# Batch 0 in four pieces, and the set-up work in another order, in a fused convolution and mixer kernel

## The chip, the cores and the metric

The kernel runs on one core of one Trainium2 chip. A core has TensorE (PE in the profile, its weight loads PEld), VectorE (DVE), ScalarE (ACT), GpSimd (POOL) and a queue for transfers (SP). The time is device microseconds of one launch; a figure for a kernel is the median of several runs.

## The reference

x has 8 batches of 4224 rows and 192 columns. The first half is a causal convolution with 7 taps; the taps of each of 8 heads (24 columns) are a softmax of its weights:

```python
w = np.exp(w - max(w)); w = w / (sum(w) + 1e-9)        # [8 heads, 7 taps]
out = np.einsum('hk,bskhg->bshg', w, x_unf)            # x_unf: the 7 rows up to s
```

The second half mixes over the rows with a low-rank product and then over the columns with two dense layers:

```python
xt = x.transpose(0, 2, 1)
h = xt @ U @ V                                         # rank 32 over the 4224 rows
u = x + h.transpose(0, 2, 1)
ch = np.maximum(u @ w_ch1, 0.0) @ w_ch2                # 192 -> 768 -> 192
return u + ch
```

Here x of the second half is the output of the first. U has 4224x32 values, V 32x4224.

## The kernel before

A batch is 33 tiles of 128 rows. In SBUF its rows lie as bf16 in two halves of the partitions (x_sb): blocks of 64 rows, 32 of them on partitions 0 to 63 (r=0) and 34 on 64 to 127 (r=1), so that tile j of a half is two neighbouring blocks. The loads convert from float32 and are all issued from GpSimd's queue.

**The convolution** is a matmul with a banded matrix. From weight the kernel makes the softmax c_sb, multiplies it with the mask hot (where the difference of row and column equals a tap), adds the seven taps by matmuls with an identity (band_half, lines 221 to 244), and copies the sums into band. conv (L368) then takes, for some heads, row halves and tiles k0 to k1, two matmuls per block (the block itself and the one before it) and evacuates the sum into y_sb by ACT ("A") or DVE ("D"), both at helper lines L272 and L274. From batch 2 on conv32 does the same with 32-row pieces and needs a shifted copy of x (xb_sb, x_shift), which GpSimd makes piece by piece.

**The low-rank part.** tt is U transposed times y: tt_mm (L403) adds 33 products, four side by side in the array; tt_split and tt_sum add the four parts with the matrix R4. h_group multiplies V with it and adds y to give u_sb; transp transposes u_sb by a transfer. **The dense part** runs over 33 groups of 8 tiles: w1 (L590) with a Relu evacuation into rl_sb, w2 (L614) with the addition of u and the store.

**The start.** Nothing of the dense part can begin before tt of batch 0 is whole. Batch 0's x comes in two pieces, KP = [(0, 13), (13, 17)] in tiles of each half, two loads per piece. GpSimd's queue, in order: piece 0, the iotas (dif four times, tap, fp, efp), U (Ur), piece 1, V0, four loads of W1, five of V, W2. U arrives as four rows side by side and is unfolded by 16 matmuls with the selection Eq (u_layout). TensorE's order: sixty matmuls of zeros (idle), the two band halves, thirty more of zeros, the convolution of piece 0 head by head, u_layout, yT_part(0) (the transposed y of group 0), tt_first (26 products, and U4_sb, the rest of U copied four times side by side by DVE), the convolution of piece 1, a float32 product that adds the four parts (R4f, L701), tt_more (7 products with U4_sb, L451), tt_done, hT_part, and then the first group of w1. Groups 0 and 1 get their transposed input from yT_part and hT_part rather than from a transfer. R4f, R4 and Eq are made on DVE after the band products (lines 250 to 265). After this start the order is written out in SLOTS: groups for w1, groups for w2, and what is done at which step of w2 (c: convolution of heads, x: shifted copy, t and s: tt and its sum, h: a group of u). Loads of later batches are held back to given points (LOADS).

Two lines carry the order of the start:

```python
    for h in range(0, H, 4):
        conv(0, h, 4, [0, 1], "AD", *KP[1])
```

Of the kernel before, what the change touches and what calls it, by code (L numbers as in the profile page):

```python
# [14 lines left out]
def kernel(  # L15
# [40 lines left out]
    def bank():  # L56
        return psp.tile([P, 512], F32, name="ps", tag="ps")
# [28 lines left out]
    KP = [(0, 13), (13, NB1 // 2)]  # L86

    def x_piece(k):
        for r in range(2):
            k0, k1 = KP[k]  # L90
            k1 = min(k1, (NB0, NB1)[r] // 2)
            x_part(0, r, (1 - r if k == 0 else 2 * k0 + 1), 2 * k1 + 1)

    x_tile(0)
    x_piece(0)
# [5 lines left out]
    dif = cst.tile([P, BW], F32, name="dif")  # L101
    for r in range(4):
        nc.gpsimd.iota(
            dif[QB * r : QB * r + QB, :],
            pattern=[[1, BW]],
            base=0,
            channel_multiplier=-1,
            allow_small_or_imprecise_dtypes=True,
        )
    tap = cst.tile([P, KC], F32, name="tap")  # L110
    nc.gpsimd.iota(
        tap[:],
        pattern=[[-1, KC]],
        base=HW,
        channel_multiplier=0,
        allow_small_or_imprecise_dtypes=True,
    )

    fp = cst.tile([P, P], I32, name="fp")
    nc.gpsimd.iota(fp[:], pattern=[[1, P]], base=P, channel_multiplier=-1)  # L120

    efp = cst.tile([P, 4, P], I32, name="efp")
    nc.gpsimd.iota(efp[:], pattern=[[-1, 4], [1, P]], base=4 * P, channel_multiplier=-4)
# [11 lines left out]
    x_piece(1)  # L135


    V0_sb = cst.tile([32, 2 * GT * P], BF16, name="V0_sb")
# [9 lines left out]
    NSL = (NT + 7) // 8 * 2  # L148
    V_sb = cst.tile([P, NSL, P], BF16, name="V_sb")
    full = NT // 8  # L150
    for q in range(4):
        src = moe_V[:, 0 : full * 8 * P].rearrange("r (k q t) -> r k q t", q=4, t=2 * P)
        nc.gpsimd.dma_start(
            out=V_sb[32 * q : 32 * q + 32, 0 : 2 * full, :].rearrange(
                "r (k a) t -> r k (a t)", a=2
            ),
            in_=src[:, :, q, :],
        )
    assert NT % 8 == 1
    nc.gpsimd.dma_start(  # L160
        out=V_sb[0:32, 2 * (NT // 8), :], in_=moe_V[:, (NT - 1) * P : NT * P]
    )
    W2_sb = cst.tile([P, MC, D], BF16, name="W2_sb")
    nc.gpsimd.dma_start(out=W2_sb[:], in_=moe_w_ch2[:].rearrange("(m p) d -> p m d", p=P))


    zz = cst.tile([P, 512], BF16, name="zz")
    nc.vector.memzero(zz[:])  # L168

    def idle(n, w):  # L170
        wps = bank()
        for _ in range(n):
            nc.tensor.matmul(  # L173
                out=wps[:, 0:w], lhsT=zz[:, 0:P], rhs=zz[:, 0:w], start=True, stop=True
            )

    idle(60, P)
# [3 lines left out]
    band = cst.tile([P, H, P], BF16, name="band")  # L181
    nc.vector.memzero(band[:])
    x_zero(0, nc.vector)
    hot = cst.tile([P, KC, BW], BF16, name="hot")
    nc.vector.tensor_tensor(
        out=hot[:],
        in0=dif[:].unsqueeze(1).to_broadcast([P, KC, BW]),
        in1=tap[:].unsqueeze(2).to_broadcast([P, KC, BW]),
        op=ALU.is_equal,
# [11 lines left out]
    nc.scalar.activation(e_sb[:], d_sb[:], ACT.Exp)  # L201
    ident = cst.tile([P, P], BF16, name="ident")
# [16 lines left out]
    HQ = H // 2  # L219

    def band_half(hh):
        pr = sml.tile([P, KC, HQ, BW], BF16, name="pr")
        nc.vector.tensor_tensor(
            out=pr[:],
            in0=hot[:].unsqueeze(2).to_broadcast([P, KC, HQ, BW]),
            in1=c_sb[:, :, HQ * hh : HQ * hh + HQ].unsqueeze(3).to_broadcast([P, KC, HQ, BW]),
            op=ALU.mult,
        )
        bp = bank()
        for d in range(KC):  # L230
            nc.tensor.matmul(
                out=bp[:, 0 : HQ * BW],
                lhsT=ident[:],
                rhs=pr[:, d, :, :],
                start=(d == 0),
                stop=(d == KC - 1),
            )
        for r in range(4):
            o = QB * (r % 2)
            nc.scalar.activation(  # L240
                out=band[QB * r : QB * r + QB, HQ * hh : HQ * hh + HQ, o : o + BW],
                in_=bp[QB * r : QB * r + QB, 0 : HQ * BW].rearrange("p (h t) -> p h t", h=HQ),
                func=ACT.Copy,
            )

    band_half(0)
    band_half(1)
# [4 lines left out]
        out=efp[:], in0=efp[:], scalar1=P - 1, scalar2=None, op0=ALU.bitwise_and  # L252
    )
    nc.vector.tensor_scalar(
        out=Eq[:], in0=efp[:], scalar1=0.0, scalar2=None, op0=ALU.is_equal
    )
# [7 lines left out]
    R4 = cst.tile([P, P], BF16, name="R4")  # L264
    nc.vector.tensor_copy(out=R4[:], in_=R4f[:])

# [9 lines left out]
    def u_layout():  # L276
        up = [bank() for _ in range(4)]
        nb = [nfull + (1 if 32 * jj < nlast else 0) for jj in range(4)]
        for a in range(4):
            for jj in range(4):  # L280
                nc.tensor.matmul(
                    out=up[jj][:, 0 : nb[jj] * R],
                    lhsT=Eq[32 * jj : 32 * jj + 32, a, :],
                    rhs=Ur[32 * jj : 32 * jj + 32, 0 : nb[jj], a * R : (a + 1) * R],
                    start=(a == 0),
                    stop=(a == 3),
                    tile_position=(32 * jj, 0),
                )
        for jj in range(4):
            evac(  # L290
                "AD"[jj % 2],
                U_sb[:, 0 : nb[jj], jj, :],
                up[jj][:, 0 : nb[jj] * R].rearrange("p (k r) -> p k r", r=R),
            )

# [38 lines left out]
    def conv32(b, h0, nh, engs):  # L334
# [5 lines left out]
        for n in range(nh):  # L340
# [3 lines left out]
            for cg in range(4):  # L344
                t, w, st = (
                    (xt[b], band[:, h, QB : 2 * QB], 1 + cg // 2)
# [21 lines left out]
    def conv(b, h0, nh, rs, engs, k0=0, k1=NT):  # L368
# [4 lines left out]
        pp = {r: bank() for r in rs}  # L373
        w = nh * GS
        for hh in range(nh):
            h = h0 + hh
            for halo in range(2):
                for r in rs:
                    for c in range(2):
# [5 lines left out]
                            lhsT=band[HB * r : HB * r + HB, h, HB * halo : HB * halo + HB],  # L385
# [42 lines left out]

    def tt_first(p, js, rest):


        U4_sb = cst.tile([P, sum(b - a for a, b in rest), 4, R], BF16, name="U4_sb")
        n = 0
        for a, b in rest:
            nc.vector.tensor_copy(
                out=U4_sb[:, n : n + b - a, :, :],
                in_=U_sb[:]
                .rearrange("p k j r -> p (k j) r")[:, a:b, :]
                .unsqueeze(2)
                .to_broadcast([P, b - a, 4, R]),  # L440
            )
            n += b - a
        p = tt_mm(0, js, p, 256)
        t = sml.tile([P, D], F32, name="tt_f", bufs=1)
        evac("A", t[:], p[:, 256 : 256 + D])
        return U4_sb, t

    def tt_more(p, U4_sb, rest):
        js = [j for a, b in rest for j in range(a, b)]
        for n, j in enumerate(js):  # L450
            nc.tensor.matmul(  # L451
                out=p[:, 0:D],
                lhsT=U4_sb[:, n, :, :].rearrange("p a r -> p (a r)"),
                rhs=yt[0][:, j, :],
                start=False,
                stop=(n + 1 == len(js)),
            )
# [84 lines left out]
    def yT_part(g):  # L542

        tp = [bank() for _ in range(3)]
        for c in range(3):
            for i in range(4):
                for hf in range(2):
                    nc.tensor.matmul(
                        out=tp[c][HB * hf : HB * hf + HB, i * P : (i + 1) * P],
                        lhsT=yt[0][:, GT * g + 4 * hf + i, HB * c : HB * c + HB],  # L550
                        rhs=ident[:],
                        start=(i == 0),
                        stop=False,
                        tile_position=(0, HB * hf),
                    )
        return tp

    def hT_part(g, tp, engs):

        uTt[g] = uts.tile([P, 4, 3, P], BF16, name="uT")  # L560
        for c in range(3):
            for hf in range(2):
                nc.tensor.matmul(
                    out=tp[c][HB * hf : HB * hf + HB, :],
                    lhsT=ttb[0][0:32, HB * c : HB * c + HB],
# [4 lines left out]
                )  # L570
            for n, eng in enumerate(engs):
# [90 lines left out]
    for k in range(5, 14):  # L662
# [3 lines left out]
        if k < 10:  # L666
# [21 lines left out]
    idle(30, P)  # L688
    for h in range(H):
        conv(0, h, 1, [0, 1], "AD", *KP[0])  # L690
    u_layout()
    yT = yT_part(0)
    jb = NB0 // 2
    rest = [(KP[1][0], jb), (jb + KP[1][0], NT)]
    ps0 = bank()
    U4_sb, tf = tt_first(
        ps0, list(range(KP[1][0])) + list(range(jb, jb + KP[1][0])), rest
    )
    for h in range(0, H, 4):
        conv(0, h, 4, [0, 1], "AD", *KP[1])  # L700
    nc.tensor.matmul(out=ps0[:, 0:D], lhsT=R4f[:], rhs=tf[:], start=True, stop=False)  # L701
    tt_more(ps0, U4_sb, rest)
# [7 lines left out]
    for r in range(4):  # L710
        q = slice(QB * r, QB * r + QB)
        nc.gpsimd.tensor_copy(
            out=band2[q], in_=band[q, :, HB * (r % 2) : HB * (r % 2) + QB]
        )
# [84 lines left out]
```

## Time and profile before

| | before |
|---|---|
| median of 7 runs | 330.98 us (329.92 to 332.28) |
| the profiled execution | 332.14 us |
| its span, first to last instruction | 330.1 us |
| TensorE busy | 319.3 us, 97% of the span |
| DVE busy | 268.5 us, 81% |
| ACT busy | 171.3 us, 52% |
| GpSimd busy | 142.0 us, 43% |
| first matmul of the first convolution | 11.43 us |
| tt_done of batch 0 (DVE L461) | 19.22 to 19.58 us |
| first matmul of w1 (L590) | 20.96 us |

The busy share is an average over stages with different limits; a matmul counts as busy until its modelled end, so a full TensorE row says that matmuls follow one another, not that each is as fast as can be. Rows of the timeline give the start, the busy time of a run of equal instructions, engine, line, output and input with their shapes and the number; in brackets the idle time before and what ended it. In the rows of a stretch each engine has its busy time and number of instructions, in the order PE, PEld, DVE, ACT, POOL; then come the granted TensorE clock, the share of the DMA engines, and GB/s.

### The profile page before, as it was taken

What the parts mean: (1) busy time and instruction counts of PE and PEld (TensorE: products, weight loads), DVE (VectorE), ACT (ScalarE), POOL (GpSimd) and SP (SyncE); (2) the same over time, 40 slices, a digit from 0 to 9 for tenths busy, and PEclk for the clock granted to TensorE, in tenths of its full rate; (3) what the DMA queues carried; (4) which work ended last, traced back from release to release, by engine and by line L of the source; (5) the groups of instructions that cost most, each with busy time, mean ns of one, the idle gap of its engine ahead of it and who ended that gap; (6) DMA issues with size and microseconds to landing.
All of it is one profiled execution on the core that took longest, in us unless ns stands there. A gap on an engine that the chain in (4) does not pass through costs nothing.

```text
span 330.1 us, 9736 instructions
## 1 busy us (share of the span) xinstructions
PE 319.3 (97%) x4072; PEld 223.8 (68%) x4072; DVE 268.5 (81%) x547; ACT 171.3 (52%) x351; POOL 142.0 (43%) x109
## 2 busy tenths in 40 slices
PE   6889999999999999999999999999999999999995
PEld 6645666667646845877784695587787487487495
DVE  5746998996985998798699789879897898896863
ACT  1648454563496088248609806842912912912910
POOL 8580329663995785969569599000000000000000
PEclk9979999999999999999999999999999999999998
DMA  8999996699999799799989979039659359249035
GB/s 101 192 171 141 172 211 149 132 185 136 286 196 182 168 177 184 163 230 155 226 180 161 188 185 224 21 114 230 83 99 228 106 124 229 82 112 271 4 120 169
DMA packets 122908, 53.54 MB, mean 162 GB/s; under 512 B 87760, under 2 KB 122832, under 8 KB 122864
## 3 DMA queue, kind: packets, MB, share of 16 engines
q1 hardware_dynamic: 84672, 38.18, 52.3%
q0 software_dynamic: 38192, 14.73, 40.3%
q8 instruction: 32, 0.52, 0.7%
q14 instruction: 12, 0.10, 0.1%
HBM read 29.49 MB, written 25.95 MB: 168 GB/s over the span
## 4 chain that ended last, share of the span: by engine, by line
PE 78%; POOL 9%; DMA 7%; DVE 2%; ACT 1%; issue 1%; POOLq 0%
PE ps L614 37%; PE ps L590 33%; DMA x_sb<-in_x_dram 6%; POOL xb_sb L318 5%; PE ps L352 3%; PE ps L496 3%; POOL x_sb L79 2%; PE ps L411 2%; ACT rl_sb L601 1%; DMA V_sb<-in_moe_V_dram 1%; DVE y_sb L274 1%; POOL xb_sb L306 1%; DVE rl_sb L603 1%; PE ps L467 0%; DVE uT L274 0%
## 5 line engine op out<-in xcount | busy, mean ns | idle before, releaser
L601 ACT ACTIVATE rl_sb<-ps 128x512 bf16<-128x512 f32 x235 | 125.5, 603 | 112.2 <-PE ps L590 100.2
L614 PE MATMUL ps<-W_sb,rl_sb 128*128 128x192 bf16 x1584 | 141.7, 246 | 0.2
L614 PEld LDWEIGHTS <-rl_sb 128*128 128x128 bf16 x1584 | 128.0, 98 | 13.4 <-issue 12.8
L590 PE MATMUL ps<-uT,W_sb 64*128 64x512 bf16 x1188 | 133.5, 380 | 0.7 <-DVE uT L274 0.7
L603 DVE TENSOR_SCALAR rl_sb<-ps 128x512 bf16<-128x512 f32 x161 | 104.3, 687 | 19.2 <-PE ps L590 18.9
L590 PEld LDWEIGHTS <-W_sb 64*128 64x128 bf16 x1188 | 64.5, 95 | 65.5 <-issue 6.6
L622 DVE TENSOR_TENSOR out_sb<-ps,u_sb 128x384 f32<-128x384 f32 (+1 forms) x133 | 70.1, 548 | 25.0 <-PE ps L614 23.5
L318 POOL COPY xb_sb<-x_sb 32x3072 bf16<-32x3072 bf16 (+1 forms) x24 | 67.6, 2824 | 0.7
L518 DVE TENSOR_TENSOR u_sb<-y_sb,ps 128x192 bf16<-128x192 bf16 (+1 forms) x168 | 66.2, 459 | 0.0
L306 POOL COPY xb_sb<-x_sb 128x3072 bf16<-128x3072 bf16 x12 | 32.7, 2742 | 29.4 <-PE ps L352 15.9
L272 ACT ACTIVATE y_sb<-ps 128x384 bf16<-128x384 f32 (+3 forms) x90 | 36.8, 502 | 10.1 <-PE ps L352 7.9
L79 POOL DMA_DIRECT2D x_sb<-in_x_dram x32 | 27.0, 851 | 29.1 <-PE ps L590 17.1
L274 DVE CAST y_sb<-ps 128x408 bf16<-128x408 f32 (+2 forms) x42 | 20.8, 547 | 3.3 <-PE ps L381 2.3
L496 PE MATMUL ps<-tt_sb,V_sb 32*128 32x192 bf16 x264 | 12.6, 246 | 0.8 <-DVE tt_sb L461 0.6
L352 PE MATMUL ps<-xb_sb,band 64*32 64x384 bf16 x192 | 12.4, 332 | 0.8 <-POOL xb_sb L318 0.8
L352 PE MATMUL ps<-x_sb,band 64*32 64x384 bf16 x192 | 12.1, 333 | 0.0
L496 PEld LDWEIGHTS <-V_sb 32*128 32x128 bf16 x264 | 4.7, 92 | 8.2 <-issue 8.2
L352 PEld LDWEIGHTS <-band 64*32 64x32 bf16 x384 | 4.6, 89 | 5.1 <-issue 4.0
L173 PE MATMUL ps<-zz 128*128 128x128 bf16 x90 | 6.8, 248 | 1.2 <-DVE zz L168 1.2
L425 ACT ACTIVATE tt_hi<-ps 128x192 bf16<-128x192 f32 x7 | 2.3, 331 | 10.8 <-PE ps L411 10.8
L381 PE MATMUL ps<-x_sb,band 64*64 64x312 bf16 (+3 forms) x192 | 7.2, 277 | 0.2 <-DMA x_sb<-in_x_dram 0.2
L173 PEld LDWEIGHTS <-zz 128*128 128x128 bf16 x90 | 6.5, 114 | 1.2 <-DVE zz L168 1.2
(64 smaller groups left out, 71.8 us busy)
## 6 DMA issues: line engine op xcount, KB each, us to landing
out_dram<-out_sb SPq DMA_DIRECT2D x131, 192.0 KB, 3.0
x_sb<-in_x_dram POOLq DMA_DIRECT2D x14, 384.0 KB, 7.9
x_sb<-in_x_dram POOLq DMA_DIRECT2D x7, 432.0 KB, 7.9
x_sb<-in_x_dram POOLq DMA_DIRECT2D x7, 408.0 KB, 7.9
x_sb<-in_x_dram POOLq DMA_DIRECT2D x1, 648.0 KB, 9.5
x_sb<-in_x_dram POOLq DMA_DIRECT2D x1, 624.0 KB, 7.1
uT<-u_sb SPq DMA_TRANSPOSE x31, 4.3
W_sb<-in_moe_w_ch_dram POOLq DMA_DIRECT2D x2, 192.0 KB, 5.8
```

The lines of the kernel that those rows point to most:

```text
L79: return nc.gpsimd.dma_start(out=xt[b][HB * r : HB * r + HB, s0:s1, :], in_=x[b, blk * HB : (blk + s1 - s0) * HB, :].rearrange("(j p) d -> ...
L272: nc.scalar.activation(out=out, in_=in_, func=ACT.Copy)
L306: nc.gpsimd.tensor_copy(out=xbt[b][:, s0:s1, :], in_=xt[b][:, s0 + 1 : s1 + 1, :])
L318: nc.gpsimd.tensor_copy(out=xbt[b][q, s0:s1, :], in_=xt[b][q, s0:s1, :])
L352: nc.tensor.matmul(out=pp[r][QB * cg : QB * cg + QB, 0 : nk[r] * GS], lhsT=w[hr], rhs=t[hr, st : st + 2 * nk[r] - 1 : 2, hs], start=True, ...
L496: nc.tensor.matmul(out=banks[pr][:, a * D : (a + 1) * D], lhsT=V_sb[32 * q : 32 * q + 32, (j // 8) * 2 + j % 2, :], rhs=ttb[b][32 * q : 32 ...
L518: nc.vector.tensor_tensor(out=u_group(g)[:, i : i + n, :, hf, :], in0=yt[b][:, run[0] : run[0] + n, :].rearrange("p n (c k) -> p n c k", c=3),
L590: last = nc.tensor.matmul(out=pp[hf][:], lhsT=W1_sb[HB * hf : HB * hf + HB, c, m * P : (m + 1) * P], rhs=uTt[g][HB * hf : HB * hf + HB, :, ...
L601: nc.scalar.activation(out=rl[:, m, hf, :], in_=pp[hf][:], func=ACT.Relu)
L603: nc.vector.tensor_scalar_max(out=rl[:, m, hf, :], in0=pp[hf][:], scalar1=0.0)
L614: nc.tensor.matmul(out=cps[:, a * D : (a + 1) * D], lhsT=rlt[g][:, m, hf, (i + a) * P : (i + a + 1) * P], rhs=W2_sb[:, m, :], start=(m == ...
L622: nc.vector.tensor_tensor(out=o[:, 0:n, :].rearrange("p n (c k) -> p n c k", c=3), in0=cps[:, 0 : n * D].rearrange("p (n c k) -> p n c k", ...
```

## The change

- Batch 0's x comes in four pieces, each of one half: 10 tiles of r=0, 10 of r=1, then 7 of r=1, then 6 of r=0. The first two are loaded at once and convolved together, two heads per evacuation; each later one by itself, three heads per evacuation, into PSUM banks that are named (work).
- Idle matmuls: five of 128x512 in float32 at the start and one between the band halves, instead of sixty and thirty of 128x128 in bf16.
- Set-up: one dif iota and an addition of 32 per row quarter instead of four iotas; hot is made after d_sb; efp is float32 and Eq compares it with a number per partition (rq); Eq and R4f are made on DVE between the products of the bands and the rest; the bands are two tiles, the second one's copies are DVE's.
- U4_sb (now 13 tiles) and R4 are made by GpSimd after u_layout, and the loads of V and W2 come behind them on GpSimd's queue.
- tt of batch 0: 20 products four side by side, then 7 late ones, the R4f product, 6 late ones. yT_part makes two of its three chunks before the later pieces and the third after the late products.
- In slot 5 the convolution of batch 3, the shifted copy of batch 4, t3 and s3 come one step of w2 later. band2 is copied in eight parts instead of four.

The core of the diff:

```diff
-    KP = [(0, 13), (13, NB1 // 2)]
+    KP = [(0, 0, 10), (1, 0, 10), (1, 10, NB1 // 2), (0, 10, NB0 // 2)]
...
-    for r in range(4):
-        nc.gpsimd.iota(
-            dif[QB * r : QB * r + QB, :],
...
+    dif = cst.tile([P, BW], F32, name="dif")
+    iota(dif[:], [[1, BW]], 0, -1)
...
-    zz = cst.tile([P, 512], BF16, name="zz")
+    zz = cst.tile([P, 512], F32, name="zz")
...
-    idle(60, P)
+    idle(5)
...
+    nc.vector.tensor_scalar(
+        out=dif[:], in0=dif[:], scalar1=rq[:, 0:1], scalar2=None, op0=ALU.add
+    )
...
-            nc.scalar.activation(
-                out=band[QB * r : QB * r + QB, HQ * hh : HQ * hh + HQ, o : o + BW],
...
+            evac(
+                "AD"[hh],
+                bands[hh][QB * r : QB * r + QB, :, o : o + BW],
...
+    band_half(0)
+    idle(1)
+    band_half(1)
...
+        if k == 5:
+            at = {
+                2: ["c3:0:3:AAD"],
+                3: ["c3:3:3:AAD"],
+                4: ["c3:6:2:A", "x4:3"],
+                5: [hs[0]],
+                6: ["t3"],
+                8: ["s3", hs[1]],
+                11: [hs[2]],
+            }
...
+    for h in range(0, H, 2):
+        conv(0, h, 2, [0, 1], "AA" if h == 0 else "AD", *KP[0][1:])
+    work = [bank() for _ in range(4)]
+    u_layout(work)
+    o = 0
+    for js in late:
+        nc.gpsimd.tensor_copy(
+            out=U4_sb[:, o : o + len(js), :, :],
...
+    nc.gpsimd.tensor_copy(out=R4[:], in_=R4f[:])
...
+    yT = yT_part(0, (0, 1))
+    ps0 = bank()
+    conv_piece(2, work[0:3])
+    conv_piece(3, [work[3], work[0], work[1]])
+    tt_mm(0, piece_tiles(0) + piece_tiles(1), ps0, 256)
+    tf = sml.tile([P, D], F32, name="tt_f", bufs=1)
+    evac("A", tf[:], ps0[:, 256 : 256 + D])
+    tt_late(ps0, late[0], 0, True, False)
+    nc.tensor.matmul(out=ps0[:, 0:D], lhsT=R4f[:], rhs=tf[:], start=False, stop=False)
+    tt_late(ps0, late[1], len(late[0]), False, True)
+    yT_part(0, (2,), yT)
     tt_done(0, ps0)
     hT_part(0, yT, "AD")
```

tt_late is the loop of tt_more for a part of the tiles; conv_piece calls conv for one half:

```python
    def conv_piece(k, pps):
        r, k0, k1 = KP[k]
        for n, h in enumerate(range(0, H, 3)):
            conv(0, h, min(3, H - h), [r], "AD"[n % 2], k0, k1, {r: pps[n]})
```

## The prediction

> **What bounds the kernel.** I read the strip of slices first, then the chain of waits, then stretches of the start.
>
> ```profile
> PE   6889999999999999999999999999999999999995
> DVE  5746998996985998798699789879897898896863
> ACT  1648454563496088248609806842912912912910
> PEclk9979999999999999999999999999999999999998
> ```
>
> TensorE is full from the third slice on; in the stretch 105:326.3 it is busy 221.24 of 221.30 us. From 105 us on nothing but its own instructions counts, and the change leaves these alone (batches 4 to 7, all groups). The change can act in two places only: until the first W1 matmul (L590, 20.96 us), and at a wait of TensorE before 105 us in slot 5. What the first W1 matmul gains, the end gains, since the evacuation-bound stretches at 30 and 41 us move along with it.
>
> The chain up to there:
>
> ```profile
> 5.28 0.86 POOL Ur L130
> 6.14 0.53 POOL Ur L134
> 6.67 0.65 POOL x_sb L79
> 7.32 8.44 DMA x_sb<-in_x_dram
> 15.76 0.28 issue
> 16.05 0.54 POOL V_sb L153
> 16.58 3.04 DMA V_sb<-in_moe_V_dram
> 19.63 0.42 PE ps L563 x2
> ```
>
> The reader sees batch 0's last rows land at 15.76. The V_sb step is how the view orders releasers; hT_part at 19.63 starts when tt_sb is written (DVE L461, 19.22 to 19.58), after the last late product of batch 0. So what ends last is: x lands, convolution, products with U, tt_done.
>
> **Part 1, the first piece and the bands.** It shrinks from 13+13 to 10+10 tiles: 53 blocks of 64 rows to 41. As bf16 in SBUF a block is 24.6 KB, so 0.295 MB less at the 190 GB/s of the slices from 4.5 us on: 1.55 us. Its second half landed at 11.94 (TensorE waits 0.19 us for it there), so now about 10.3. The bands must be as early. Before, hot waited until 4.60 for the four dif iotas; one iota is left (0.65 us less), and hot moves behind d_sb, where DVE would wait for ACT's exp. The first pr goes from 6.71 to about 5.9 and ends at 7.1. The first half's seven products and four ACT copies (2.45 us for eight) end at 9.2 to 9.7; the second half's copies go to DVE and end near 11, when heads 4 to 7 are wanted. So the convolution starts at 10.3 instead of 11.94.
>
> What could take that back stands ahead of the band products in TensorE's order: five float32 matmuls of 128x512 instead of sixty bf16 ones of 128x128 (4.94 us). The nearest row is
>
> ```profile
> 17.76 0.59 PE L701 MATMUL ps<-tt_f,R4f 128*128 128x192 f32 x2
> ```
>
> with the next matmul 0.54 us after its start, at full clock. It has two records of at least 326 ns, against 246 ns for one bf16 matmul of 192 columns: 80 ns of streaming more each, so twice the columns per record. By that streaming 512 columns need 4 x 512 columns, 0.85 us; with the weight loads (two of 0.19 us, partly hidden) about 1.0. Scaled by columns whole, 1.44 is the other bound. The granted clock reads 1.00 from the start, but 29 of the sixty short matmuls fill the 3.01 us up to 4.21 and the other 31 take 1.93 us: 104 ns and 62 ns each, so about half rate until 4.2 us. At 1.0 the five end at 7.7 (1.4 to 4.2 us hold 1.4 of them), at 1.44 near 9.9. I take 1.0. The cover is x's landing: ends up to about 8.8 cost nothing, after that microsecond for microsecond.
>
> **Part 2, from there to tt_done.** The first convolution has 8 evacuations of 480 columns instead of 16 of 312. ACT's eight of 312 took 2.69 us and eight of 384 2.69+0.50=3.19, so 0.875 ns a column and 0.48 us each; DVE (3.21 us for eight of 312, 3.99 for eight of 408) 0.57. Five on ACT end at about 13.4; u_layout runs under them, its four evacuations (0.38 to 0.41) end at 14.1; yT for two of three chunks (16 at 28 ns) stands in between; piece 2 (7 tiles of the second row half) runs 14.0 to 15.1, its x due about 13.6. Then TensorE waits for piece 3. Piece 3 is the last of batch 0's x; all bytes ahead of it are those of before (pieces and U, 1.87 MB), so it lands where the last landed before: 15.2 (bytes over the slices' rate, plus 0.9 us from last byte to landing) to 15.76. I take 15.6. **This is the point of the whole start:** TensorE gains 1.6 us at the front and meets the same landing.
>
> From there, in TensorE's order:
> - piece 3: 32 matmuls of 144 columns, two side by side in the array (one half of the rows). yT's 24 of 128 columns took 0.86 us, 28 ns apart; so 31 ns, 1.0 us
> - 20 products with U, four side by side: the 26 of L411 are 22 ns apart, 0.44 us
> - seven late products: L451's are 95 ns apart, 0.67; tt_f's evacuation (0.33, and 0.4 of latencies around it) lies beside them. It reads the PSUM bank that they write; no row of before shows the two together. If they wait for it, 0.65 more; I take nothing, as their columns differ (0 to 191, 256 to 447)
> - the float32 R4f product 0.54, six late products 0.57, then latency of the last and start of DVE, 0.25.
>
> Sum 3.5 us: tt_done at 19.1, against 19.22 before. There x was already there when TensorE was still at yT and the first products (until 16.95), and only 7 late products came after it; now 13 do, and the whole of piece 3. Gain 0.1; by the landing (15.2 to 15.76) and the shared bank between 0.5 gained and 0.8 lost. yT's third chunk, 0.2 us, lies under tt_done.
>
> **Part 3, GpSimd.** U4 (7+6 tiles, 128 columns each) goes from DVE (0.35 and 0.28 us for 3 and 4 tiles) to GpSimd, and R4 with it. Row: a 3072-column bf16 copy takes 2742 ns there, 0.89 ns a column, so 1664 columns 1.5 us plus R4 0.25. The skill's "GPSIMD Engine Reference", section Key points, says that elementwise work is about twice as fast on DVE: from DVE's 0.63 us for 7 tiles, 1.2 for 13, the rule gives 2.4. By the row the copies end at 15.9, by the rule at 16.8; the late products start at 17.1. Hidden by both; past 17.1 each microsecond counts. But behind them on GpSimd's queue stand five V loads, W2 (0.88 us) and batch 1's x. V starts at 16.0 instead of 14.18. Until 18.5 the DMA engines still work off W1, so they don't run dry; V is first used at 28.3, W2 at 33.5, x of batch 1 at 41.95, whose landing goes from 31 to at most 33. Costs nothing. band2 in eight copies is first used at 71 us. Eq and R4f stand between the band products on DVE, 0.5 us and ready long before u_layout.
>
> **Part 4, slot 5.** The convolution of batch 3 moves back by one W2 step.
>
> ```profile
> 97.07 3.08 POOL L318 COPY xb_sb<-x_sb 32x3456 bf16<-32x3456 bf16 x1
> 100.20 0.33 PE L352 MATMUL ps<-xb_sb,band 64*32 64x408 bf16 x1 [0.78 <-POOL xb_sb L318]
> ```
>
> TensorE arrived at 99.09 and waited 0.78 us for GpSimd's last shifted copy. A W2 step (12 matmuls) takes 1.10 us, so it now arrives at about 100.2, when the copy is done: 0.78 gone. Next late is the tile sums, which keep their two steps from t to s and three to the group that needs them; the shift for batch 4 starts 1.1 us later and GpSimd has 3.21 us idle at 113.4. Gain 0.78, bounds 0.5 to 0.8.
>
> **The clock.** A second term lies in the start:
>
> ```profile
> 17.86:21.28 3.42, 2.40 (x17) 1.22 (x18) 1.86 (x6) 1.33 (x5) 3.42 (x6) 1.00 1.21 142
> 21.28:24.69 3.41, 3.41 (x19) 1.41 (x18) 0.99 (x2) 1.68 (x3) 2.43 (x6) 0.50 1.59 190
> ```
>
> The eighth column is the granted clock: 0.50 for 3.41 us after a stretch with TensorE busy for 2.40 of 3.42, and twice the time for W1 there: 1.7 us lost. The Trainium skill, "TensorE: Matmul & The Clock Gate", section Why this matters for your kernels, asks for no idle gaps above some 3 us; no gap here reaches 1 us, so by it this term is zero, and the row says 1.7 us. Its Part 1 says that the window runs freely against the kernel's start, which fits the seven times: three at 329.9 to 330.5, one at 331.0, three at 332.0 to 332.3. The gaps about hT_part stay, less 0.2 us of yT, so I leave its frequency as it was and count from the median.
>
> **Sum.** The profiled execution took 332.14 us (span 330.1 and 2.0 around it). Less 0.1 and 0.78 it would be 331.3 with the lowered clock, 329.6 without. Against the median of 330.98: 330.98 - 0.88 = **330.1**.
>
> **Rivals.**
> - **Nothing gained, 330.9.** The landing of piece 3 at 15.8 or later, or the late products wait for tt_f. For: TensorE meets the same landing. Against: slot 5's wait is read from the trace and goes by itself. 14%.
> - **More gained, 329.0.** Piece 3 lands at 15.2 (0.5 us) and the lowered clock comes in fewer executions, a further 0.5 to 1.2 in the median. For: piece sizes and yT's filler; against: the gaps at 19.1 and 20.3 are unchanged. 20%.
> - **Slower, 333.0: the clock at the start.** The five float32 matmuls end after 8.8 us. If they do not raise the clock, each takes 1.9 us, they end at 10.9, the bands at 13, piece 3 follows at 17.8 instead of 15.6, and what follows runs at half rate for a while: +2.8, less 0.78. It decides from 9.8 us on (1.0 past the cover outweighs slot 5's gain). For: sixty plus thirty short matmuls kept TensorE busy until 11.3 and few remain; against: the array streams as densely in float32. 18%.
>
> **How the numbers follow.** The forecast has 48%, with its own range 329.1 to 331.3. A difference of about 0.5% (1.65 us) can be told from no change. Of the forecast's 48, 10 are below 329.33; with the second rival's 20 that gives 0.30 faster. Slower, above 332.63: 16 of the third rival and 1 of the forecast, 0.17. Same 0.53. The range from 328.6 to 332.5 leaves the worst of the third rival and a little of the second out.
>
> **What would show it.** TensorE's first convolution matmul at about 10.3; a wait for x before piece 3 near 15.1; tt_done at 19.1; W1 at 20.85; no wait for xb_sb at the convolution of batch 3; the five float32 matmuls over by 8 us. Wrong if W1 starts before 20.3 or after 21.5, or if TensorE gets a new wait after 21 us.

## The result, and the profile after

| | before | after |
|---|---|---|
| median | 331.10 us (61 runs, 329.69 to 333.17) | 329.71 us (24 runs, 329.38 to 331.12) |
| ratio after to before | | 0.9958, 95% interval 0.9944 to 0.9972 |
| profiled execution, its span | 332.14 us, 330.1 us | 330.22 us, 328.4 us |
| first matmul of w1 | 20.96 us | 20.27 us |
| from there to the end of the last matmul | 305.29 us | 303.30 us |
| from there to the landing of the last store | 1.97 us | 2.87 us |

The kernel is faster by 1.39 us, 0.42%, which is real but under 0.5%. The three lower rows are read from the traces' instruction and transfer records. The strip of slices of the kernel after:

```profile
PE   8989999999999999999999999999999999999994
DVE  6738999996978987898798799879888888896852
ACT  1758444662576198078429708824904903903900
PEclk9999999999999999999999999999999999999999
```

The first two slices of TensorE are fuller (8 and 9 for 6 and 8), and the clock has lost its 7 in the third. The rest is as before. The start in the timeline of the kernel after:

```profile
1.47 6.81 PE L155 MATMUL ps<-zz 128*128 128x512 f32 x10 [1.47 <-DVE zz L145]
8.11 0.62 PE L232 MATMUL ps<-pr,ident 128*128 128x152 bf16 x7
...
10.03 1.11 PE L367 MATMUL ps<-x_sb,band 64*64 64x240 bf16 x34
...
11.50 1.01 PE L367 MATMUL ps<-x_sb,band 64*64 64x240 bf16 x30 [0.36 <-DVE band L254]
...
13.60 2.27 PE L367 MATMUL ps<-x_sb,band 64*64 64x168 bf16 x64
...
14.17 1.69 POOL L683 COPY U_sb<-U_sb 128x896 bf16<-128x896 bf16 x2 [2.04 <-DVE U_sb L254]
...
15.81 0.29 POOL L691 CAST R<-R4f 128x128 bf16<-128x128 f32 x1
...
16.83 0.74 PE L664 MATMUL ps<-y_sb,U_sb 128*128 128x192 bf16 x7 [0.43 <-ACT tt_f L252]
...
18.52 0.36 DVE L419 CAST tt_sb<-ps 128x192 bf16<-128x192 f32 x1 [2.22 <-PE ps L664]
...
20.27 1.92 PE L550 MATMUL ps<-uT,W_sb 64*128 64x512 bf16 x14 [0.50 <-DVE uT L254]
```

The convolution starts at 10.03 and, in the row at 13.60, pieces 2 and 3 run as 64 matmuls in one go: TensorE waits for no x at all. Two new waits stand there, 0.36 us for the second band half and 0.43 us for tt_f. The chain of waits of the same execution, from its beginning, no longer holds a landing of x:

```profile
1.47 6.81 PE ps L155 x10
8.27 0.46 PE ps L232 x7
...
11.50 1.01 PE ps L367 x30
...
13.66 2.20 PE ps L367 x64
```

It starts at the float32 idle matmuls and runs to w1 through TensorE and evacuations. So the start is bound by something else than before, and the experiments come back to it. The stretches of the clock, at the same times as before:

```profile
17.86:21.28 3.42, 2.74 (x29) 1.33 (x28) 1.44 (x4) 0.94 (x3) 3.42 (x6) 1.00 0.80 83
21.28:24.69 3.41, 3.41 (x40) 1.68 (x36) 1.46 (x3) 3.35 (x7) 3.29 (x9) 1.00 1.49 175
```

TensorE is busy 2.74 instead of 2.40 us in the first, and the clock (eighth column) stays at 1.00 in the second. In slot 5, the timeline shows the last shifted copy over at 96.70 and the convolution running from 98.39 with no wait; before, the copy ended at 100.15 and TensorE waited 0.78 us:

```profile
93.62 3.08 POOL L303 COPY xb_sb<-x_sb 32x3456 bf16<-32x3456 bf16 x1
...
96.30 2.15 PE L574 MATMUL ps<-W_sb,rl_sb 128*128 128x192 bf16 x24
98.39 0.35 PE L337 MATMUL ps<-xb_sb,band 64*32 64x384 bf16 x2
```

One profile against the other, the difference is made of these parts: w1 starts 0.69 earlier; the lowered clock is absent, 1.71 (half of its 3.41); slot 5, 0.78; a new wait of 0.46 us for uT at 36.27, in this execution and not in the next one of the same kernel; and the last store, 0.90 later after the last matmul. The sum is -1.82 against -1.72 between the spans. The medians move by less, because before has the lowered clock only in some executions.

### The profile page after: what moved, and what is told of

The parts are those of the page before. It is cut to its first block, busy times and chain, and to the rows that moved or that the text cites. A ratio compares the mean times of both kernels' runs of the same rounds, so it can differ in the third digit from the quotient of the medians.

```text
span 328.4 us, 9588 instructions
## 1 busy us (share of the span) xinstructions
PE 319.0 (97%) x3994; PEld 221.0 (67%) x3994; DVE 268.9 (82%) x552; ACT 170.3 (52%) x346; POOL 143.8 (44%) x113
## 4 chain that ended last, share of the span: by engine, by line
PE 89%; DVE 5%; DMA 2%; ACT 2%; issue 0%; DVEq 0%
PE ps L574 40%; PE ps L550 37%; PE ps L337 3%; PE ps L454 3%; PE ps L155 2%; DMA uT<-u_sb 2%; PE ps L399 2%; ACT rl_sb L561 1%; DVE rl_sb L563 1%; DVE u_sb L476 1%; PE ps L367 1%; DVE y_sb L254 1%; DVE uT L254 0%; DVE band L254 0%; DVE out_sb L582 0%
## 5 line engine op out<-in xcount | busy, mean ns | idle before, releaser
L550 PE MATMUL ps<-uT,W_sb 64*128 64x512 bf16 x1188 | 132.0, 376 | 1.2 <-DVE uT L254 0.8
L291 POOL COPY xb_sb<-x_sb 128x3072 bf16<-128x3072 bf16 x12 | 32.7, 2743 | 29.6 <-PE ps L337 21.7
L252 ACT ACTIVATE y_sb<-ps 128x408 bf16<-128x408 f32 (+4 forms) x89 | 37.7, 512 | 10.1 <-PE ps L337 7.8
L254 DVE CAST y_sb<-ps 128x408 bf16<-128x408 f32 (+4 forms) x37 | 19.7, 577 | 1.0 <-PE ps L367 1.0
L155 PE MATMUL ps<-zz 128*128 128x512 f32 x12 | 7.9, 809 | 1.5 <-DVE zz L145 1.5
L367 PE MATMUL ps<-x_sb,band 64*64 64x240 bf16 (+3 forms) x192 | 7.8, 276 | 0.4 <-DVE band L254 0.4
L367 PEld LDWEIGHTS <-band 64*64 64x64 bf16 x192 | 5.9, 106 | 2.0 <-issue 1.0
```

The source lines that it names most:

```text
L252: nc.scalar.activation(out=out, in_=in_, func=ACT.Copy)
L291: nc.gpsimd.tensor_copy(out=xbt[b][:, s0:s1, :], in_=xt[b][:, s0 + 1 : s1 + 1, :])
L550: last = nc.tensor.matmul(out=pp[hf][:], lhsT=W1_sb[HB * hf : HB * hf + HB, c, m * P : (m + 1) * P], rhs=uTt[g][HB * hf : HB * hf + HB, :, ...
```

## The experiments

Each ratio is to the kernel before on the same chip, in the same set of runs. A profile is one execution; "W1" is its first w1 matmul, "body" the time from there to the end of the last matmul. In the kernel before the body is 303.6 us where slot 5 waits and the clock isn't lowered (305.29 - 1.71); without either it is 302.8. "Lowered" counts runs with a mean granted clock of 0.995 or less. One stretch of 3.41 us at 0.50 takes 0.005 off the mean over 330 us. The fall of the clock after the last matmul takes up to 0.004 (e2's profile, which has no such stretch, reads 0.996), so the two kinds of runs lie close, but hardly mix.

| kernel | median us (runs) | ratio, 95% | W1 | body | store after | lowered |
|---|---|---|---|---|---|---|
| c0, changed kernel again | 330.10 (12) | 0.9975, 0.9953 to 0.9998 | 20.35 | 302.86 | 2.91 | 0 of 12 |
| e1, its slot 5 undone | 330.14 (21) | 0.9966, 0.9950 to 0.9981 | 20.83 | 302.81 | 2.96 | 0 of 21 |
| e2, its yT whole and early | 330.09 (11) | 0.9953, 0.9934 to 0.9971 | 21.00 | 302.78 | 2.90 | 0 of 11 |
| e3, its tt_f in a bank of its own | 329.95 (14) | 0.9954, 0.9930 to 0.9978 | 19.52 | 302.79 | 2.78 | 1 of 14 |
| e5, its idle matmuls as before | 330.46 (12) | 0.9990, 0.9972 to 1.0008 | 21.64 | 302.81 | 2.46 | 0 of 12 |
| e6, sixteen idle DVE instructions more | 328.71 (12) | 0.9948, 0.9929 to 0.9966 | 21.09 | 302.80 | 1.93 | 0 of 12 |
| e8, e3 and e6 together | 329.15 (12) | 0.9951, 0.9930 to 0.9972 | 19.66 | 303.05 | 1.93 | 0 of 12 |
| e4, before with yT's third chunk late | 330.89 (22) | 0.9987, 0.9969 to 1.0004 | 21.80 | 303.63 | 1.96 | 0 of 22 |
| e7, before with wide idle matmuls | 335.16 (4) | 1.0102, 1.0072 to 1.0132 | 23.54 | 305.75 | 1.95 | 4 of 4 |
| e9, before with the new slot 5 | 331.68 (10) | 0.9994, 0.9970 to 1.0018 | 21.42 | 302.79 | 1.97 | 7 of 10 |
| e10, before with pieces 10 and 7 or 6 | 330.72 (10) | 0.9966, 0.9944 to 0.9987 | 21.26 | 303.45 | 1.97 | 0 of 10 |
| e11, before with eight idle DVE instructions | 330.43 (10) | 0.9973, 0.9947 to 0.9998 | 20.98 | 302.66 | 3.25 | 2 of 10 |

The kernel before itself had the lowered clock in 18 of 55, 13 of 35 and 14 of 25 runs of the three sets, 45 of 115 together. Its runs without it have medians of 330.75, 330.50 and 330.44 us; the first set goes with e1 to e4, the second with c0, e5, e6 and e8, the third with the rest.

c0 is the changed kernel once more, beside e5, e6 and e8 on one chip.

> The changed kernel once more, as the yardstick for the three others on the same chip: median 329.5 to 330.0. Its wait of 0.5 us for a transposed u at 36 us is either there again (then batch 1's later loads cause it) or not (then it is a matter of the single execution); its last store ends 2.8 to 3.0 us after the last matmul again if that belongs to the program.

It gave 330.10, and its profile shows the parts of above again: W1 at 20.35, no wait in slot 5, the last store 2.91 us after the last matmul; the wait for uT is not there. Against the runs of before without the lowered clock it gains 0.40 us (330.10 to 330.50). The parts in its profile give as much: 0.61 from W1 and 0.74 from the body, less 0.94 for the store, are 0.41.

### Slot 5: the move alone, and all but the move

e9 puts the new order of slot 5 into the kernel before; e1 takes the same lines out of the changed kernel.

```diff
-        if k < 10:
+        if k == 5:
+            at = {
+                2: ["c3:0:3:AAD"],
+                3: ["c3:3:3:AAD"],
+                4: ["c3:6:2:A", "x4:3"],
...
+        elif k < 10:
```

> The kernel before with slot 5's move alone. As predicted for the change: the wait of 0.6 to 0.8 us for xb_sb goes, from the first W1 matmul to the last matmul 302.8 us (303.6 before without a lowered clock), median 0.6 to 0.8 below before, 330.3. If a later step takes it back: the wait goes, that stretch stays at 303.6.

> The changed kernel with slot 5 as before (batch 3's convolution after the first W2 step). If slot 5's wait goes by the move alone: the wait for xb_sb is back at about 0.8 us in the profile and the median is 0.6 to 0.8 us above the changed kernel (330.4). If the shifted copies would have been in time anyway in the changed start: no wait, median 329.7.

e9: the body is 302.79, 0.8 us under the 303.6, and the wait is gone. The time does not show it: seven of its ten runs have the lowered clock, and the three others took 330.25, 330.38 and 330.58, where such runs of before have 330.44. That it was the move, and not an earlier copy, the traces show: the last copy ends 77.33 us after W1 in e9, and 77.53 and 77.35 in e4 and e10, where TensorE waits 0.64 and 0.46 us for it. The timeline of TensorE in e9 (w2 groups, then the convolution with no bracket):

```profile
96.94 2.16 PE L614 MATMUL ps<-W_sb,rl_sb 128*128 128x192 bf16 x24
99.03 0.35 PE L352 MATMUL ps<-xb_sb,band 64*32 64x384 bf16 x2
```

e1 missed: with slot 5 as before the wait did not come back. The last copy, a w2 group and the convolution in e1's timeline:

```profile
94.24 3.08 POOL L303 COPY xb_sb<-x_sb 32x3456 bf16<-32x3456 bf16 x1
...
96.82 0.82 PE L574 MATMUL ps<-W_sb,rl_sb 128*128 128x192 bf16 x8
97.57 0.35 PE L337 MATMUL ps<-xb_sb,band 64*32 64x384 bf16 x2
```

The copies follow the landing of batch 3's x (the copy over all 128 partitions, L291 there and L306 before, waits for it): that copy starts 59.1 us after W1 in e1 and 59.0 in the changed kernel, 59.9 in e9 and 61.8 before, of which 1.7 are the lowered clock. So in the changed kernel the x lands about a microsecond earlier against w1. The last copy ends 75.9 to 76.6 us after W1 in the eight profiles of it and its variants, and TensorE, in the old order, wants it at 76.7 (e1). Either cause removes the same wait: by the profiles the move is worth 0.8 us to the kernel before and nothing to the changed one. e11's profile, of the kernel before, has no such wait either (58.8 us).

Why the x comes earlier stays open, but the traces show what goes with it. The load of batch 3's last piece takes 11.5 to 11.9 us from issue to landing in before, e4, e9 and e10, and 9.1 to 10.8 in the ten other profiles. In those four a 16 KB instruction fetch of 1.9 to 2.4 us lies beside it, and in the ten others none is longer than 1.5. Whether the fetch holds up the load, or both are slow for one reason, is not shown.

### The lowered clock: what stands in the stretch before it

The changed kernel has more work for TensorE around tt_done: yT's third chunk, and thirteen late products instead of seven. e4 moves only the chunk, in the kernel before; e2 undoes only the chunk, in the changed one; e10 changes only the sizes of the pieces before, which makes thirteen late products (and takes three heads per evacuation of the second piece instead of four).

```diff
-    yT = yT_part(0)
+    yT = yT_part(0, (0, 1))
...
+    yT_part(0, (2,), yT)
     tt_done(0, ps0)
```

> The kernel before with one thing of the change: yT's third chunk after the late products. Theory clock: few or no executions with the lowered clock, spread 329.7 to 331 instead of 329.7 to 333.2, median about 330.3, 0.8 below before. Theory start: spread as before, median within 0.3 of 331.1.

> The changed kernel with all three chunks of yT made before the later pieces, so that nothing stands between the last late product and hT_part. Theory clock (the filled gap around hT_part keeps the clock up): some executions, up to half, have the clock at half for 3.4 us again, times spread up to 331.5, median 0.3 to 0.9 above the changed kernel. Theory start (the gain comes from earlier work alone): spread and median as the changed kernel, within 0.3, or up to 0.2 slower because yT's 0.2 us is no longer under tt_done.

```diff
-    KP = [(0, 13), (13, NB1 // 2)]
+    KP = [(0, 10), (10, NB1 // 2)]
...
-    for h in range(0, H, 4):
-        conv(0, h, 4, [0, 1], "AD", *KP[1])
+    for h in range(0, H, 3):
+        conv(0, h, min(3, H - h), [0, 1], "AD", *KP[1])
```

> The kernel before with pieces of 10+10 and 7+6 tiles alone (three heads per evacuation of the second). By the prediction's part 2 the smaller first piece meets the same landing of the last x and has 13 late products: W1 at 20.6 to 21.5, median within 0.5 of before. If the landing does not bind: W1 up to 0.7 earlier.

The lowered clock comes in 0 of 22 runs of e4 and 0 of 10 of e10, against 45 of 115 of the kernel before; e2 has none in 11. So the late chunk is enough by itself (e4), and so are the other piece sizes (e10), which bring the larger late part. The time shows no more than that: e4's 330.89 and e10's 330.72 are not below the 330.75 and 330.44 of before's runs without the lowered clock, and the 330.3 expected of e4 did not come. e4's lowest busy time over any 3.41 us of this part is 2.73, against 2.39 before; the row of stretches in e4:

```profile
18.39:21.80 3.41, 2.73 (x45) 1.61 (x34) 1.84 (x5) 1.59 (x5) 3.41 (x6) 1.00 0.97 108
```

The busy share alone does not decide, though. The clock changes in whole steps of 3.41 us from its rise: in the kernel before the lowered clock began five steps, 17.07 us, after the rise at 4.21, in e7 again 17.07, and in all fourteen traces the fall after the last matmul comes 94, 95 or 96 whole steps after the rise. Here are e2 and e10 in the stretch that these steps give, four after the rise:

```profile
18.78:22.20 3.42, 2.40 (x21) 0.99 (x20) 1.44 (x4) 1.07 (x4) 3.42 (x7) 1.00 0.89 96
```

```profile
18.24:21.66 3.42, 2.40 (x24) 1.44 (x23) 1.27 (x5) 0.94 (x3) 3.28 (x6) 1.00 1.14 124
```

Both are busy for 2.40 us as before was, and stayed at full clock afterwards (e9's 2.44 too). Stretches with less work did so as well, like the first one after the rise in the kernel before (1.93 us):

```profile
4.21:7.62 3.41, 1.93 (x34) 1.81 (x32) 2.67 (x9) 0.25 (x1) 3.34 (x8) 1.00 1.51 178
```

In e7 the stretch at 16.27, with 2.21 us, was not followed by a lowered clock, and the next one, with 2.33, was:

```profile
19.69:23.10 3.41, 2.33 (x23) 1.35 (x24) 0.95 (x3) 0.86 (x3) 3.25 (x6) 1.00 1.32 153
```

Nor is it the number of matmuls: 17 before and 23 in e7, but 21 and 24 in e2 and e10. What else decides stays open. It differs from run to run of one program: e9 has the lowered clock in 7 of 10 runs and e11 in 2 of 10, with the same work of TensorE in this part. The price of one lowered stretch is the difference of the medians of the two groups of runs of before: 1.5, 1.5 and 2.1 us in the three sets; the profile gave 1.7.

e7 belongs to slot 5: it was to see whether fewer instructions on TensorE at the start move the fetches, bring the landing of batch 3's x forward and so end the wait there: fifteen and eight idle matmuls of 512 columns instead of sixty and thirty of 128.

```diff
-    idle(60, P)
+    idle(15, 512)
...
-    idle(30, P)
+    idle(8, 512)
```

> The kernel before with its idle matmuls as 15 and 8 of 512 columns instead of 60 and 30 of 128: the same time on TensorE, 134 instructions fewer in its program, so that its 16 KB instruction loads fall elsewhere. Theory fetch (such a load, 2.3 us long beside batch 3's x, delays the shifted copies): the last copy of batch 3 is done at least 0.7 earlier against the third slot's W1, the wait for xb_sb is gone or below 0.2, median 0.5 to 0.8 below before. Theory that something else delays them: the wait stays at 0.6 to 0.8, median as before.

The wait in slot 5 is gone, and the load of batch 3's last piece took 9.75 us instead of 11.86, beside a fetch of 0.93. But the gain in time missed, with a median of 335.16. TensorE stood still for 1.70 us in the middle of the second piece's convolution, with nothing in the trace that it waited for (timeline of TensorE in e7):

```profile
20.19 0.28 PE L381 MATMUL ps<-x_sb,band 64*64 64x72 bf16 x8 [1.70 <-issue]
...
23.54 2.74 PE L590 MATMUL ps<-uT,W_sb 64*128 64x512 bf16 x12 [0.50 <-DVE uT L274]
```

w1 starts 2.6 us later and all four runs have the lowered clock. And a wait of 1.57 us like that of slot 5 stands three batches later, at 187.67 us: there the loads took 12.9 to 13.4 us, beside two fetches of 1.6 and 1.9. So the profile agrees with the expectation that slow loads and long fetches go together, without showing which is the cause; before has a fetch of 2.1 us at 97.92 beside loads of 6.2 and 6.5. The cause of the stop stays open too: a 16 KB fetch begins at 17.71 us, just ahead of it, but before has one at 18.68 with no stop.

### The start: the bank of tt_f, and the idle matmuls

e3 lets the 20 products go into a PSUM bank of their own, from which tt_f is evacuated, so that the late products share nothing with it.

```diff
-    tt_mm(0, piece_tiles(0) + piece_tiles(1), ps0, 256)
+    tt_mm(0, piece_tiles(0) + piece_tiles(1), work[2], 0)
...
-    evac("A", tf[:], ps0[:, 256 : 256 + D])
+    evac("A", tf[:], work[2][:, 0:D])
```

> The changed kernel with the first 20 products in a PSUM bank of their own, so that the late products need not wait for tt_f's evacuation. If the wait of 0.43 us on ACT tt_f is a matter of the shared bank and the start is bound by TensorE: the wait is gone, W1 starts about 0.4 earlier (19.85) and the median falls by 0.3 to 0.5. If R4f, which needs tt_f as well, only waits later instead: W1 0.0 to 0.1 earlier, median unchanged.

The wait is gone: the late products follow the 20 in the timeline of e3, 0.53 us from start to start instead of 1.03.

```profile
14.49 1.19 PE L367 MATMUL ps<-x_sb,band 64*64 64x144 bf16 x32 [0.17 <-DMA x_sb<-in_x_dram]
15.61 0.60 PE L399 MATMUL ps<-y_sb,U_sb 128*32 128x192 bf16 x20
16.14 0.75 PE L664 MATMUL ps<-y_sb,U_sb 128*128 128x192 bf16 x7
```

w1 starts at 19.52 in this execution, and the profiled run is at 328.85. The median does not show it (329.95, between the changed kernel's 329.71 and 330.10): 0.43 us is below what a dozen runs tell apart, and the moment at which the clock rises, next, moves the start by more.

e5 gives the changed kernel its old idle matmuls, sixty and thirty of 128x128 in bf16.

```diff
-    zz = cst.tile([P, 512], F32, name="zz")
+    zz = cst.tile([P, 512], BF16, name="zz")
...
-    idle(5)
+    idle(60)
...
-    idle(1)
+    idle(30)
```

> The changed kernel with the idle matmuls of before (sixty and thirty of 128x128 in bf16, the thirty between the band halves). Theory warm-up neutral: W1 starts within 0.3 of the changed kernel, median within 0.3. Theory that the float32 matmuls delay the bands in executions whose clock rises late: spread of the times narrower, median 0.2 to 0.4 lower; against that the thirty hold the second band half 1 us longer, up to 0.5 higher.

Its median is 0.36 us above c0's, with overlapping intervals. In its profile TensorE waits 0.85 and 0.17 us for x, as pieces 2 and 3 land at 14.5 and 16.0, though they were issued at the same times as in c0. So nothing is settled on the edit. It shows how far the landing of the same bytes moves from execution to execution: issued at 6.5 us, piece 3 took 8.0 us to land in c0, 8.1 after, 8.9 in e2 and 9.5 in e5.

What does move the start of the changed kernel is when the clock rises. In e3 the weight loads of the float32 idle matmuls come 0.85 us apart until 4.2 and 0.43 us apart later; in e6 until 7.6 (PEld rows of both timelines; columns: start, length):

```profile
3.33 0.34 PEld L155 LDWEIGHTS ps<-zz 128*128 128x128 f32 x1 [0.52 <-issue]
4.18 0.32 PEld L155 LDWEIGHTS ps<-zz 128*128 128x128 f32 x1 [0.52 <-issue]
4.74 0.19 PEld L155 LDWEIGHTS ps<-zz 128*128 128x128 f32 x1 [0.24 <-issue]
5.17 0.19 PEld L155 LDWEIGHTS ps<-zz 128*128 128x128 f32 x1 [0.24 <-issue]
```

```profile
6.75 0.34 PEld L157 LDWEIGHTS ps<-zz 128*128 128x128 f32 x1 [0.52 <-issue]
7.60 0.23 PEld L157 LDWEIGHTS ps<-zz 128*128 128x128 f32 x1 [0.52 <-issue]
8.07 0.19 PEld L157 LDWEIGHTS ps<-zz 128*128 128x128 f32 x1 [0.24 <-issue]
```

One such matmul is two records, so 1.7 us at half rate and 0.86 at full. From the clock's records (rise) and the timelines of seven executions with the float32 idle matmuls:

| us | e3 | e8 | e2 | after | c0 | e1 | e6 |
|---|---|---|---|---|---|---|---|
| rise of the clock | 4.43 | 5.07 | 5.13 | 6.04 | 6.20 | 7.16 | 7.67 |
| band half 0 starts | 7.37 | 7.64 | 7.67 | 8.11 | 8.19 | 8.67 | 8.93 |
| W1 | 19.52 | 19.66 | 21.00 | 20.27 | 20.35 | 20.83 | 21.09 |

The bands move by half of the rise: (8.93 - 7.37) / (7.67 - 4.43) = 0.48. In the four executions on the right, which share the tt_f wait and have no wait for x, W1 moves with it: (21.09 - 20.27) / (7.67 - 6.04) = 0.50. (e3 and e8 lack the tt_f wait, and e2 waits 0.70 us for x of the first piece.) The kernel before is not moved like that: W1 is at 20.96 with a rise at 4.21, and at 20.98 in e11 with a rise at 7.11, since there x's landing ends last.

### The tail: where the last store lands

The last two stores (96 KB each) take longer to land after the change. The lists of transfers in the last microseconds, with the median from issue to landing at the end of the row, first before, then after, then e6:

```profile
out_dram<-out_sb SPq DMA_DIRECT2D x2, 96.0 KB, 1.8
```

```profile
out_dram<-out_sb SPq DMA_DIRECT2D x6, 192.0 KB, 2.2
out_dram<-out_sb SPq DMA_DIRECT2D x2, 96.0 KB, 2.8
```

```profile
out_dram<-out_sb SPq DMA_DIRECT2D x6, 192.0 KB, 2.0
out_dram<-out_sb SPq DMA_DIRECT2D x2, 96.0 KB, 1.7
```

In the trace after, an instruction fetch of 8 KB (queue q14) starts 0.86 us after the last matmul, while the stores are under way; before, it comes at 3.56 us, when they have landed. The trace does not name a packet's DMA engine. But after the change the last store packets end one by one, about 0.03 us apart, from 2.17 to 2.88 us, as if one engine were behind, while before all are through at 1.97. VectorE has 552 busy instructions instead of 547 after the change. If the fetch is that of VectorE's program, some instructions more or less on VectorE move it. e6 puts sixteen one-column writes of zeros at the start of VectorE's work, where it has time, and e11 eight of them into the kernel before:

```diff
+    for _ in range(16):
+        nc.vector.memset(rq[0:QB, 0:1], 0.0)
```

> The changed kernel with sixteen more tiny memsets on DVE in the set-up, 0.8 us where DVE waits for the first iota. Theory fetch (an 8 KB instruction load, which DVE's longer program puts beside the last stores, holds one DMA engine and with it the last store): the load moves about 16 DVE instructions forward, the last store ends 2.0 us after the last matmul instead of 2.9, median 0.7 to 0.9 lower. Otherwise: last store at 2.9 as before, median within 0.2.

> Own PSUM bank for the first 20 products and the sixteen memsets together, as a candidate that beats both: 0.9 for the last store and 0.3 to 0.5 for the bank below the changed kernel, 328.3 to 328.8; without the fetch theory 329.3 to 329.6.

> The kernel before with eight tiny memsets more on DVE, at a place where DVE waits 2.8 us. Theory fetch: DVE's program is now as long as the changed kernel's, the 8 KB instruction load falls beside the last stores, the last store ends 2.8 to 3.0 us after the last matmul instead of 2.0, median 0.7 to 0.9 above before (331.8). Otherwise: 2.0 and the median of before.

| | before | e11 | after | c0 | e6 | e8 |
|---|---|---|---|---|---|---|
| fetch, us after the last matmul | 3.56 | 0.69 | 0.86 | 0.69 | -6.66, then 3.51 | -6.72, then 3.53 |
| last store, us after the last matmul | 1.97 | 3.25 | 2.87 | 2.91 | 1.93 | 1.93 |

The padding moves the fetch both ways as expected, and the last store goes with it: 0.98 us better in e6 against c0, 1.28 worse in e11 against before. The other traces agree. In seven (after, c0, e1, e2, e3, e5, e11) the fetch starts 0.7 to 1.3 us after the last matmul, and the last store lands at 2.46 to 3.25; in the other seven no fetch does, and it lands at 1.93 to 1.97. The fetch is not all of it: e5 loses only 0.5 us with a fetch at 0.70, and in e11 the last store was also issued later, 1.74 us after the last matmul instead of 0.61.

e6's first pr is at 6.04 as in c0, so its padding costs nothing; its later W1 is the late rise of its clock (1.47 us later than in c0, half of it is 0.74). In the time, e6 is 1.39 us below c0 on the same chip, 328.71 to 330.10, and ten of its twelve runs are below the fastest of c0's; that is more than the 0.98 of the store, and the rest may be the draw of the clock's rise. e11's median is not higher than before's (330.34 to 330.44 in the runs without the lowered clock): its profile has no wait in slot 5, which makes up for much of the late store. e6 has the lowest median of all and beats both kernels' medians; e8's, with tt_f's bank added, is 329.15, and its ratio is no different from e6's.

## Why the prediction was right or wrong

330.1 was forecast, 329.71 came. The effect was taken at -0.88 us and measured at -1.39. That the sum came so near is in good part luck: terms that it had wrong or left out cancelled.

- **Slot 5, -0.78: right in the kernel before.** e9's profile shows 303.6 going to 302.8 with the wait gone. But e1 shows that in the changed kernel the x comes early enough without the move; the term is not to be added to the others there.
- **The start, -0.1: the path was wrong, the size is not settled.** It was "the point of the whole start" that TensorE meets the same landing of piece 3 at 15.6. It did not: piece 3 was there by 14.6 after, 14.5 in c0 and e3, 15.4 in e2, 16.0 in e5. The 15.2 to 15.76 were one execution's landing carried over; 1.87 MB of packets on that queue were done at 13.75 instead of 14.01 us, and landing followed by 0.85 instead of 1.75. W1 gained 0.69 after and 0.61 in c0. But in e1 and e6, with the same order of TensorE, it is at 20.83 and 21.09: the four profiles have 20.64 in the mean, and the three of the old start (before, e9, e11) 21.12. So some 0.5 us, within a scatter of 0.8, and the 20.85 of the forecast lies inside it.
- **"I take nothing" for tt_f's bank: wrong.** The late products waited 0.43 us, inside the bound of 0.65, though their columns differ; e3 removes it with another bank.
- **The five float32 matmuls: rightly sized, their cover wasn't.** 0.86 us each at full clock and 1.7 at half, against 1.0 and 1.9; the first band product came at 8.11 after, in seven executions between 7.37 and 8.93. "Ends up to about 8.8 cost nothing" failed: the first piece landed at about 9.7 (issued at 2.3, 7.4 us) instead of 10.3, so the chain of waits runs through these matmuls, and w1 comes 0.5 us later for each microsecond that the clock rises later. The rise at 4.2 was taken from one execution, and was the earliest of all that were profiled. The rival that made this 2.8 us slower did not come: the float32 matmuls do raise the clock.
- **The second band half: 11.50 for 11.** It cost 0.36 us, since the convolution of the first heads was over at 11.14.
- **GpSimd's copies: right.** 1.69 us for 1664 columns and 0.29 for R4, over at 16.10, near the 15.9 of the row of the trace; the Trainium skill's rule ("GPSIMD Engine Reference", Key points) gave 2.4 us for these columns and 16.8 for the end, too slow here.
- **The clock, "I leave its frequency as it was": this step failed.** It went from 45 of 115 runs to none in 36 of the changed kernel. "The gaps about hT_part stay" overlooked what else stands in the stretch: yT's third chunk and six more late products. At 1.5 to 2.1 us each, 39% of the runs is 0.6 to 0.8 us of the mean. In before's median it is 0.3, 0.4 and 1.5 us in the three sets; the last one has it in more than half of its runs. The rule of the Trainium skill that was weighed ("TensorE: Matmul & The Clock Gate", Why this matters for your kernels: no idle gap above some 3 us) was kept by the kernel before, whose longest gap in that stretch was 0.52 us, and the clock fell all the same: the row decides. The window running freely against the kernel's start (Part 1 there) agrees with rises between 4.21 and 7.67 us in these traces, and with every later change of the clock a whole number of 3.41 us after the rise.
- **The end: missed altogether.** The sum let the span follow the last matmul. The last matmul came 2.68 us earlier, the span shrank by 1.72, mainly since the last store landed 0.90 later, with an instruction fetch beside it.

The mark "wrong if W1 starts before 20.3" was passed by 0.03 us after and by 0.8 in e3. The other mark, a new wait of TensorE after 21 us, came in the profile after (0.46 us for uT at 36.27) and not in c0; its cause is open. "More gained" named both halves that came, an earlier piece 3 and a rarer lowered clock; its 329.0 was not reached, and e6, whose last store lands as early as before's, took 328.71.

## What to carry to other kernels

Take a landing, or the moment at which the clock rises, from several executions before making it the point on which a sum turns; a chain that passes from a landing to TensorE's own first matmuls inherits the time that they run at half rate. Count what fills the few microseconds before a lowered clock, not only its gaps: a late chunk of eight matmuls was enough to keep it away. And look at what ends after the last matmul: eight or sixteen instructions on an engine with time to spare put an instruction fetch beside the last stores or away from them.

## What the runs showed of the hardware

- In the kernel before the clock was lowered to 0.50 for one stretch of 3.41 us, 17.07 us after its rise, with no gap of TensorE above 0.52 us in the stretch before; of 115 runs of the same program 45 had it. A stretch with the same busy time (2.40 us of 3.41) went without in e2 and e10, and one with less (1.93) in the same trace.
- Every change of the clock in the fourteen traces lies a whole number of 3.41 us after its rise, and the rise lies between 4.21 and 7.67 us.
- A float32 matmul of 128x512 is two records of 0.43 us each at full clock, 0.85 at half.
- With an instruction fetch of 8 KB 0.7 to 1.3 us after the last matmul, the last store landed at 2.46 to 3.25 us (seven traces), without one at 1.93 to 1.97 (seven).
- The same bytes (piece 3), issued at the same time, landed between 8.0 and 9.5 us after issue in executions of kernels with the same loads.
